# More places for the first attention pairs, and a planner that paces its transfers

## The chip, the cores and the metric

The kernel runs on one core of one Trainium2 chip. The metric is device time in microseconds (us) of one execution. TensorE is called PE below, its weight loads PEld; VectorE is DVE, ScalarE ACT, GpSimd POOL, SyncE SP.

## The reference

Attention with 4 batches, 8 heads, 768 positions and 64 channels, in float32. A position sees the 96 keys before it (itself included) and the 8 first keys of its batch. The result, 3072 rows of 512, goes through a two-layer network with a cosine gate.

```python
scores = scale * np.matmul(q, k.transpose(0, 1, 3, 2))
keep = is_global | is_local            # first 8 keys, or 0 <= rel < 96
scores = np.where(keep, scores + bias, -1e9)
a = np.exp(scores - max);  a = a / (a.sum(-1) + 1e-9)
x = np.matmul(a, v)                    # reshaped to (3072, 512)
h = x @ w_in                           # (3072, 2048)
out = (h * np.cos(h)) @ w_out          # (3072, 512)
```

## The kernel before

The 3072 rows are eight **chunks** of 384 (two for each batch). A chunk's attention is four **pairs** of heads; each pair gives 128 of the 512 columns of x. Numbered over all chunks there are 32 pairs.

A pair goes through these steps (the functions are `plan_loads`, `plan_unit`, `plan_values`): queries and keys arrive in a place of class `raw`, values in a place of class `v` (L438, L441); PE makes scores into a bank (L521 for the first eight pairs, in plain float32; L525 for the others, whose queries and keys are first split into two parts by `plan_split`, into a place of class `qk`); DVE folds (L538), adds distances and takes the minimum into a tile `tt` (L547); ACT takes exponentials (L572); DVE or POOL normalises (L595, L600); PE transposes (L664); DVE masks into a tile `pv` (L672, L677); PE multiplies by the values (L699); x is written in two parts, `xh` and `xl` (L253, L720).

The network is 128 **steps**, in each one block of 128 of the 2048 inner columns for one chunk. A step has 12 matmuls over x (L735, three for each pair's part of x, into one of two banks `ph`), then ACT L752, DVE L755, ACT L758 (cosine), DVE L793 (**the product**, after which the bank `ph` is free), a copy `gh` and DVE or POOL L802 `gl`, and at last 9 matmuls by w_out (L746). The order of the steps is in `PHASES`: chunk 0 with blocks 0 to 7, chunk 1 with blocks 0 to 15, chunk 0 with blocks 8 to 15, then the other chunks with all 16.

The weights arrive as 64-bit floats in 32 **tiles** of 512 KB (L372, 16 of w_in and 16 of w_out), and each is turned into two float32 parts by six operations on ACT, DVE and POOL (`plan_weights`; on DVE always the join L399, and at times L385 and L409).

The order on every engine is written by a planner at build time (`Plan.run`). It holds a list of operations with costs, due times and the places that each uses, and picks on each engine, in simulated time, the operation with the earliest due time that has its inputs and a free place. An operation that has a place of a class holds it until its last user is through. A place class has a list of names, `NT, NST, NPV, ...` of them; a name stands for a buffer. For SP the planner counts 470 ns for issuing a transfer, after which SP is free for the next; the data come later, one transfer behind the other (`extra`). Engines run what is written in that order. Where PE would stand idle in the first 45000 ns of the plan, matmuls of zeros are put in (`idle`, L1039).

A general fallback that stands behind the plan in the program is not run with these inputs.

## Time and profile before

| | us |
|---|---|
| three runs | 712.12, 712.63, 714.5 (median 712.63) |
| the profiled execution's own time | 714.17 |
| its span, from first to last instruction | 712.4 |
| PE busy | 688.6 (97%) |
| DVE busy | 518.8 (73%) |
| ACT busy | 450.9 (63%) |
| POOL busy | 135.8 (19%) |

The shares are means over the whole span. PE's busy time holds matmuls of zeros too. The rows on which the prediction rests stand in a section below, word for word.

### The profile page before, as it was taken

To read this page: it belongs to the slowest core of one execution; us is meant where nothing else is said; L and a number is where in the kernel's file an instruction comes from. 1 tells how busy PE (TensorE), PEld (TensorE's weight loads), DVE (VectorE), ACT (ScalarE), POOL (GpSimd) and SP (SyncE) were. 2 spreads that over 40 slices of the span, in tenths; PEclk is the share of its full clock that TensorE was granted. 3 is DMA by queue.
4 is the path that set the end of the run, shared out by engine and by line. 5 is a ranking of instruction groups with operands and counts; after the bars stand their busy time and mean duration, and the time that the engine had idled before them with its cause. 6 is when DMAs were issued, how large, how long until landed. Compare 5 with 4: busy or idle time off the path is not lost.

```text
span 712.4 us, 12947 instructions
## 1 busy us (share of the span) xinstructions
PE 688.6 (97%) x4483; PEld 598.4 (84%) x4483; DVE 518.8 (73%) x1542; ACT 450.9 (63%) x1130; POOL 135.8 (19%) x166
## 2 busy tenths in 40 slices
PE   7898999999999999999999999999999999999996
PEld 3657878988888888889889898888888888899884
DVE  7999999898767778487775887667785877743332
ACT  5799977786756576466664667566764666634342
POOL 4715656530002121011000121011000112000000
PEclk8999999999999999999999999999999999999999
DMA  8997210022420322132230422203122310001001
GB/s 303 407 351 209 59 48 24 1 59 64 112 68 29 83 65 65 48 103 60 56 71 15 112 61 58 59 19 106 42 68 67 90 49 2 1 1 45 1 0 50
DMA packets 32603, 55.74 MB, mean 78 GB/s; under 512 B 3472, under 2 KB 18192, under 8 KB 32528
## 3 DMA queue, kind: packets, MB, share of 16 engines
q1 hardware_dynamic: 32528, 54.82, 26.4%
q8 instruction: 37, 0.61, 0.4%
q14 instruction: 38, 0.31, 0.1%
HBM read 48.52 MB, written 6.29 MB: 77 GB/s over the span
## 4 chain that ended last, share of the span: by engine, by line
PE 72%; DVE 11%; ACT 8%; issue 2%; DMA 1%; POOL 0%; ACTq 0%; DVEq 0%; POOLq 0%; SPq 0%
PE bank L735 31%; PE bank L746 30%; PE bank L699 5%; PE bank L525 3%; ACT tt L572 2%; PE bank L664 2%; DVE wu L399 1%; ACT rr L758 1%; ACT L572 1%; DVE w L409 1%; DVE tt L547 1%; DVE gl L802 1%; DVE rr L755 1%; DVE qs L623 1%; DMA raw<-in_qk_dram 1%
## 5 line engine op out<-in xcount | busy, mean ns | idle before, releaser
L735 PE MATMUL bank<-xh,w 128*128 128x384 f32 x1024 | 298.1, 343 | 4.3 <-DVE rr L793 4.3
L746 PE MATMUL bank<-w,gh 128*128 128x512 f32 x768 | 243.6, 398 | 0.0
L735 PEld LDWEIGHTS bank<-xh,w 128*128 128x128 f32 x1024 | 189.1, 189 | 12.0 <-DVE rr L793 5.8
L735 PE MATMUL bank<-xl,w 128*128 128x384 f32 x512 | 173.3, 339 | 0.8 <-DVE xl L720 0.8
L746 PEld LDWEIGHTS bank<-w,gh 128*128 128x128 f32 x768 | 138.4, 188 | 21.5 <-ACT raw L394 0.3
L746 PE MATMUL bank<-w,gl 128*128 128x512 f32 x384 | 151.9, 396 | 0.0
L755 DVE SCALAR_TENSOR_TENSOR rr<-rr,bank 128x384 f32<-128x384 int32 x129 | 69.8, 542 | 102.6 <-ACT rr L752 102.2
L752 ACT ACTIVATE rr<-bank 128x384 int32<-128x384 f32 x129 | 62.1, 482 | 127.5 <-PE bank L735 124.5
L758 ACT ACTIVATE rr<-rr,half_pi 128x384 f32<-128x384 f32 x129 | 78.4, 613 | 43.0 <-DVE rr L755 41.4
L735 PEld LDWEIGHTS bank<-xl,w 128*128 128x128 f32 x512 | 96.8, 189 | 5.4 <-DVE xl L720 1.4
L793 DVE TENSOR_TENSOR rr<-bank,rr 128x384 f32<-128x384 f32 x129 | 70.5, 551 | 41.2 <-ACT rr L758 40.6
L572 ACT ACTIVATE tt<-tt,st 96x104 f32<-96x104 f32 (+1 forms) x256 | 94.2, 369 | 7.0 <-DVE st L547 6.4
L746 PEld LDWEIGHTS bank<-w,gl 128*128 128x128 f32 x384 | 72.1, 188 | 16.7
L257 POOL TENSOR_SCALAR ks<-raw 128x408 fp32r<-128x408 f32 (+1 forms) x35 | 21.1, 602 | 308.6 <-PE bank L525 291.6
L802 DVE TENSOR_TENSOR gl<-rr,gh 128x384 fp32r<-128x384 f32 (+1 forms) x113 | 65.9, 583 | 7.7 <-ACT gh L253 5.5
L253 ACT CAST gh<-rr 128x384 fp32r<-128x384 f32 (+1 forms) x99 | 50.2, 508 | 29.0 <-DVE rr L793 20.5
L547 DVE CUSTOM_DVE_ANT_0 tt<-bank,dd 96x104 f32<-96x104 f32 (+1 forms) x256 | 55.7, 257 | 3.0
L699 PEld LDWEIGHTS bank<-pv,v 104*64 104x64 f32 (+1 forms) x960 | 42.1, 138 | 12.5 <-issue 8.0
L525 PEld LDWEIGHTS bank<-ks,qs 128*96 128x96 f32 x384 | 45.8, 162 | 5.3 <-issue 0.8
L699 PE MATMUL bank<-pv,v 104*64 104x96 f32 (+1 forms) x960 | 48.3, 252 | 0.8 <-DMA raw<-in_qk_dram 0.4
L525 PE MATMUL bank<-ks,qs 128*96 128x200 f32 (+1 forms) x384 | 47.9, 255 | 0.5 <-DVE st L547 0.5
L572 ACT ACTIVATION_READ_ACCUMULATOR tt<-tt,st 96x1 f32 x256 | 47.9, 187 | 0.0
(96 smaller groups left out, 727.0 us busy)
## 6 DMA issues: line engine op xcount, KB each, us to landing
raw<-in_qk_dram SPq DMA_DIRECT2D x48, 224.0 KB
raw<-in_qk_dram SPq DMA_DIRECT2D x48, 198.0 KB
raw<-in_w_in_dram SPq DMA_DIRECT2D x16, 512.0 KB
raw<-in_w_out_dram SPq DMA_DIRECT2D x16, 512.0 KB
out_dram<-oo SPq DMA_DIRECT2D x24, 256.0 KB
v<-in_v_dram SPq DMA_DIRECT2D x16, 240.0 KB
v<-in_v_dram SPq DMA_DIRECT2D x16, 192.0 KB
raw<-in_qk_dram SPq DMA_DIRECT2D x4, 448.0 KB
```

The source lines that it names most:

```text
L253: self.nc.scalar.copy(out, x)
L525: nc.tensor.matmul(out, qs[:, m, q0], ks[:, k : k + w], start=m == 0, stop=m == 1)
L547: nc.vector.tensor_tensor_reduce(tt[t // 2].tile[:, t % 2, j, :w], ps.tile[:R, i * WIN : i * WIN + w], self.dd[:, v, :w], op0=ALU.add, op1 ...
L572: nc.scalar.activation(x, x, AF.Exp, bias=st.tile[:, c : c + 1], scale=-1.0, accum_out=st.tile[:, n2 + c : n2 + c + 1])
L699: nc.tensor.matmul(px.tile[j * D : (j + 1) * D, t * R : (t + 1) * R], vs.tile[:k, t + c, hs][:, j * D : (j + 1) * D], pv[:k, c, o : o + R] ...
L735: self.nc.tensor.matmul(ph[:, :CW], self.wi[f][:, w, kk * P : (kk + 1) * P], xx[:, kk, :], start=kk == 0 and m == 0, stop=kk == self.NK - ...
L746: self.nc.tensor.matmul(po, gg[:, ts], self.wo[f][:, w, :], start=start and m == 0, stop=stop and m == 2)
L752: self.nc.scalar.activation(r.bitcast(I32), ph, AF.Copy, scale=1.0 / TWO_PI, bias=0.25)
L755: self.nc.vector.scalar_tensor_tensor(r, r.bitcast(I32), -TWO_PI, ph, op0=ALU.mult, op1=ALU.add)
L758: self.nc.scalar.activation(r, r, AF.Sin, bias=self.half_pi)
L793: {DVE: dve}, lambda e, r=r, h=h: nc.vector.tensor_tensor(r(), h(), r(), op=ALU.mult), [o], [ph, rr]
L802: self.eng(e).tensor_tensor(g[1][:, cs], r(), g[0].bitcast(F32)[:, cs], op=ALU.subtract)
```

## The change

1. The first pairs may use more places. `HOMES = 7`: for the first seven pairs the classes `tt`, `v` and `pv` become `ttearly`, `vearly`, `pvearly`. `ttearly` is the five `tt` places and the two key places `k0`, `k1`; `vearly` is the three `v` places and the query place `q0`; `pvearly` the three `pv` places and `q1`. These four are otherwise first needed by the ninth pair.
2. For this the class `qk` is taken apart into `q` and `k`.
3. `NST` (statistics tiles) goes from 3 to 5.
4. `DEPTH = 3000`: in the plan SP is free again only when the transfers that have been issued end within 3000 ns.

```diff
-NT, NST, NPV, NX, NV, NRAW, NQK, NRR, NG = 5, 3, 3, 2, 3, 3, 2, 3, 2
+NT, NST, NPV, NX, NV, NRAW, NQK, NRR, NG = 5, 5, 3, 2, 3, 3, 2, 3, 2
+DEPTH = 3000
+HOMES = 7
...
                     if e == SP:
                         dma = max(end + 300, dma) + o.extra
+                        self.free[SP] = max(end, dma - DEPTH)
+                        heapq.heappush(heap, self.free[SP])
                         end = dma + 1400
...
+    def early(self, cls, n, pr):
+        return f"{cls}early" if n * self.NP + pr < HOMES else cls
...
-        vs = Slot("v", lambda i: self.work.tile([SLOT, 1 + CT, W], F32, name="v", tag=i))
+        vs = Slot(self.early("v", n, b2), lambda i: self.work.tile([SLOT, 1 + CT, W], F32, name="v", tag=i))
...
-        qk = Slot("qk", lambda i: [
-            self.work.tile([P, 2, CW], F32R, name="qs", tag=f"q{i}"),
-            self.work.tile([P, KW], F32R, name="ks", tag=f"k{i}"),
-        ])
+        qq = Slot("q", lambda i: self.work.tile([P, 2, CW], F32R, name="qs", tag=i))
+        kk = Slot("k", lambda i: self.work.tile([P, KW], F32R, name="ks", tag=i))
...
-                "tt": names("tt", NT), "st": names("st", NST), "qk": names("qk", NQK), "raw": names("raw", NRAW),
-                "v": names("v", NV), "pv": names("pv", NPV), "x": names("x", NX),
+                "tt": names("tt", NT), "st": names("st", NST), "q": names("q", NQK), "k": names("k", NQK), "raw": names("raw", NRAW),
+                "v": names("v", NV), "pv": names("pv", NPV), "ttearly": names("tt", NT) + names("k", 2),
+                "vearly": names("v", NV) + ["q0"], "pvearly": names("pv", NPV) + ["q1"], "x": names("x", NX),
```

The change moves instructions on every engine until about the 28th step; the last 102 products and what DVE does between them, and the last 101 steps on PE, stand in the same order as before. In the changed kernel the lines are 6 to 13 higher (L746 is the old L735, L757 the old L746, L710 the old L699, L675 the old L664, L534 the old L521, L444 and L447 the old L438 and L441, L493 the old L483, L378 the old L372).

On SP, before, the values of the fourth pair (`v`, 96x4x128) stand behind 18 of the 32 weight tiles:

```order
L372 DMA raw<-in_w_out_dram 128x1024 x3
L483 DMA raw<-in_qk_dram 128x896
L372 DMA raw<-in_w_out_dram 128x1024
L372 DMA raw<-in_w_in_dram 128x1024 x2
L438 DMA v<-in_v_dram 96x4x128
L441 DMA v<-in_v_dram 8x3x128
L372 DMA raw<-in_w_in_dram 128x1024 x2
```

On SP now:

```order
L444 DMA v<-in_v_dram 96x4x128
L378 DMA raw<-in_w_in_dram 128x1024
L493 DMA raw<-in_qk_dram 128x792
L447 DMA v<-in_v_dram 8x3x128
L444 DMA v<-in_v_dram 96x4x128
L447 DMA v<-in_v_dram 8x3x128
L378 DMA raw<-in_w_in_dram 128x1024 x3
L378 DMA raw<-in_w_out_dram 128x1024
L493 DMA raw<-in_qk_dram 128x896
```

The fourth pair's values (the second `v` here) now stand behind one weight tile. The queries and keys of the fifth to eighth pair (`raw`, 128x896) stand behind 5, 7, 10 and 12 tiles now; before, behind 5, 13, 27 and 31.

On PE, before, around the values' product of the fourth pair (L699, the fourth of its kind), which ends chunk 0's attention:

```order
L1039 MATMUL idle<-zeros 128x512
L699 MATMUL bank<-pv,v 64x96 x14
L521 MATMUL bank<-raw 96x200 x4
L664 MATMUL bank<-ident,tt 104x96 x4
L735 MATMUL bank<-xh,w 128x384
L735 MATMUL bank<-xl,w 128x384
```

On PE now, at the same place:

```order
L710 MATMUL bank<-pv,v 64x96 x14
L534 MATMUL bank<-raw 96x200 x4
L675 MATMUL bank<-ident,tt 96x96 x2
L675 MATMUL bank<-ident,tt 104x96 x6
L746 MATMUL bank<-xh,w 128x384
L746 MATMUL bank<-xl,w 128x384
L746 MATMUL bank<-xh,w 128x384 x2
L746 MATMUL bank<-xl,w 128x384
L746 MATMUL bank<-xh,w 128x384 x2
L746 MATMUL bank<-xl,w 128x384
L746 MATMUL bank<-xh,w 128x384
L710 MATMUL bank<-pv,v 64x96 x14
```

Now the fourth L710 follows the third with half a pair's scores, the fourth pair's transposes and nine matmuls of the first step between. Before, two and a half more score groups, the transposes, 18 step matmuls and 33 matmuls of zeros stand between the third and the fourth. In all there are 65 matmuls of zeros before and 30 now.

What DVE has ahead of it changes so (instructions on DVE ahead of four places, before and now; the two bold names are the product L793 and the last `xl` of a chunk, L720):

| DVE instruction (old line) | 4th **xl** | 5th **product** | 8th **product** | 11th **product** |
|---|---|---|---|---|
| fold L538 | 22, 18 | 24, 32 | 32, 32 | 32, 32 |
| minimum L547 | 44, 33 | 48, 64 | 64, 64 | 64, 64 |
| normalise L600 (L595) | 6, 4 (6, 4) | 8, 11 (6, 4) | 11, 11 (6, 4) | 11, 11 (6, 4) |
| mask L672 and L677, each | 9, 8 | 12, 14 | 16, 16 | 16, 16 |
| xl L720 | 4, 4 | 5, 7 | 7, 8 | 8, 8 |
| weights: join L399 | 8, 3 | 13, 13 | 16, 16 | 21, 18 |
| weights: L409 (L385) | 6, 1 (3, 1) | 7, 9 (4, 2) | 9, 11 (5, 2) | 11, 13 (8, 2) |
| gl L802 | 0, 0 | 3, 2 | 3, 5 | 6, 7 |
| query rest L623 | 0, 0 | 0, 0 | 0, 0 | 2, 0 |
| copies L255 and L490 | 0, 0 | 4, 2 | 8, 3 | 9, 4 |
| small L563, L580, L583, each | 5, 4 | 6, 7 (8, 8) | 8, 8 | 8, 8 |

On POOL there are 14 more instructions in all: 10 of them for weights (five of these L388), four for normalising. On ACT the table for exponentials or cosines is loaded 9 times ahead of the fifth cosine, 3 times before.

## Rows read from the trace of the kernel before

**Rows 1.** The page, its first part: busy time of each engine, its share of the span, and instructions.

```profile
PE 688.6 (97%) x4483; PEld 598.4 (84%) x4483; DVE 518.8 (73%) x1542; ACT 450.9 (63%) x1130; POOL 135.8 (19%) x166
```

**Rows 2.** Busy time by stretch. Columns: stretch and length, busy time of PE, PEld, DVE, ACT and POOL with their instructions, granted clock of TensorE (1.00 is 2.4 GHz), share of the DMA engines, GB/s.

```profile
0.00:38.00 38.00, 30.55 (x236) 19.75 (x237) 32.81 (x135) 26.11 (x91) 21.28 (x50) 0.91 0.97 350
38.00:57.00 19.00, 14.69 (x103) 8.44 (x103) 18.56 (x69) 17.77 (x48) 5.25 (x6) 1.00 1.04 370
0.00:74.37 74.37, 62.61 (x451) 43.95 (x451) 67.56 (x232) 59.87 (x171) 36.76 (x64) 0.93 0.89 304
0.00:113.64 113.64, 100.97 (x722) 75.04 (x722) 105.03 (x329) 91.40 (x246) 60.94 (x84) 0.95 0.66 219
57.68:61.10 3.42, 3.42 (x13) 3.42 (x11) 2.93 (x8) 3.03 (x12) 0.82 (x1) 0.50 1.09 264
20.00:57.68 37.68, 30.98 (x247) 19.92 (x246) 36.78 (x127) 34.26 (x99) 17.40 (x18) 1.00 1.04 380
114.24:704.00 589.76, 586.26 (x3755) 522.58 (x3756) 413.07 (x1211) 357.38 (x882) 74.30 (x83) 1.00 0.19 51
```

**Rows 3.** PE in order of time, from 38 us to the first L746. Columns: start and length in us, what it is, how many in the row, idle time before it and who ended that.

```profile
40.56 4.49 PE L1039 MATMUL idle<-zeros 128*128 128x512 bf16 x20
45.66 0.99 PE L521 MATMUL bank<-raw 64*96 64x200 f32 x8 [0.60 <-ACT raw L488]
46.58 0.54 PE L664 MATMUL bank<-ident,tt 96*104 96x96 f32 x4
46.96 2.11 PE L1039 MATMUL idle<-zeros 128*128 128x512 bf16 x9
48.99 1.39 PE L699 MATMUL bank<-pv,v 96*64 96x96 f32 x28
...
56.84 0.44 PE L735 MATMUL bank<-xh,w 128*128 128x384 f32 x1 [3.70 <-DVE rr L793]
...
62.67 0.62 PE L746 MATMUL bank<-w,gh 128*128 128x512 f32 x2
```

**Rows 4.** PE in order of time, the two last stops of more than half a us before the end of the start-up.

```profile
102.49 0.44 PE L735 MATMUL bank<-xl,w 128*128 128x384 f32 x1 [0.83 <-DVE xl L720]
...
114.24 0.44 PE L735 MATMUL bank<-xh,w 128*128 128x384 f32 x1 [0.63 <-DVE rr L793]
```

**Rows 5.** SP in order of time: issues of the fourth pair's values and of the last three `raw` loads of the first eight pairs.

```profile
23.61 0.33 SPq L483 DMA_DIRECT2D raw<-in_qk_dram  x1
...
28.70 0.33 SPq L438 DMA_DIRECT2D v<-in_v_dram  x1
...
45.45 0.35 SPq L483 DMA_DIRECT2D raw<-in_qk_dram  x1
...
54.07 0.35 SPq L483 DMA_DIRECT2D raw<-in_qk_dram  x1
```

**Rows 6.** DVE in order of time: the fourth xl, the fifth product and its successor, the eighth product, the eighth xl, the eleventh product with the join ahead of it.

```profile
51.35 0.58 DVE L720 TENSOR_TENSOR xl<-bank,xh 128x384 fp32r<-128x384 f32 x1
...
74.37 0.54 DVE L793 TENSOR_TENSOR rr<-bank,rr 128x384 f32<-128x384 f32 x1
74.83 0.55 DVE L755 SCALAR_TENSOR_TENSOR rr<-rr,bank 128x384 f32<-128x384 int32 x1
...
96.88 0.54 DVE L793 TENSOR_TENSOR rr<-bank,rr 128x384 f32<-128x384 f32 x1
...
101.90 0.54 DVE L720 TENSOR_TENSOR xl<-bank,xh 128x384 fp32r<-128x384 f32 x1
...
112.16 1.56 DVE L399 SCALAR_TENSOR_TENSOR wu<-raw 128x512 uint32<-128x512 uint32 x1
113.64 0.54 DVE L793 TENSOR_TENSOR rr<-bank,rr 128x384 f32<-128x384 f32 x1
```

**Rows 7.** Groups of DVE, one of POOL and three of ACT by line and shape, whole span. Columns: how many, busy time in us and mean ns of one, idle time before them and who ended it.

```profile
L547 DVE CUSTOM_DVE_ANT_0 tt<-bank,dd 96x104 f32<-96x104 f32 x224 | 50.0, 257 | 2.1
L538 DVE COPY_PREDICATED bank<-mine,bank 96x192 f32<-96x192 uint32 x96 | 32.9, 352 | 1.6 <-PE bank L521 0.8 <-PE bank L525 0.6
L388 POOL TENSOR_SCALAR raw<-raw 128x512 bf16<-128x512 bf16 x24 | 34.9, 1501 | 0.2
L600 DVE TENSOR_TENSOR tt<-tt,st 96x416 f32<-96x416 f32 x39 | 28.8, 754 | 0.1
L672 DVE TENSOR_TENSOR pv<-bank,others 104x384 f32<-104x384 f32 x48 | 26.2, 546 | 0.8 <-PE bank L664 0.8
L399 DVE SCALAR_TENSOR_TENSOR wu<-raw 128x512 uint32<-128x512 uint32 x32 | 24.6, 780 | 0.0
L409 DVE TENSOR_TENSOR w<-wu,w 128x512 fp32r<-128x512 f32 x17 | 13.2, 783 | 0.5 <-ACT w L253 0.5
L385 DVE TENSOR_SCALAR raw<-raw 128x512 uint16<-128x512 uint16 x8 | 6.0, 776 | 0.0
L572 ACT ACTIVATE tt<-tt,st 96x104 f32<-96x104 f32 x224 | 82.5, 369 | 4.0 <-DVE st L547 3.6
L572 ACT ACTIVATION_READ_ACCUMULATOR tt<-tt,st 96x1 f32 x256 | 47.9, 187 | 0.0
L758 ACT ACT_TABLE_LOAD x28 | 35.9, 1283 | 0.5
```

**Rows 8.** PE's steady prices, from the chain that ended last. Columns: start, us, what, how many.

```profile
114.24 2.35 PE bank L735 x12
116.59 2.08 PE bank L746 x9
118.67 2.12 PE bank L735 x12
120.80 2.09 PE bank L746 x9
232.35 1.48 PE bank L699 x32
```

**Rows 9.** The joins L399 and the normalising L600 on DVE over the span: shortest, median and longest in ns, first and last start.

```profile
L399 DVE SCALAR_TENSOR_TENSOR wu<-raw x32: 673/682/1559, 24.7 to 153.9; 128x512 uint32<-128x512 uint32 x32
L600 DVE TENSOR_TENSOR tt<-tt,st x39: 575/582/1746, 12.3 to 614.2; 96x416 f32<-96x416 f32 x39
```

More of the change, by code (lines that the diff above doesn't have):

```diff
@@ L268, in constants @@
         make_identity(nc, self.ident)
-        tile3 = lambda name, **kw: self.const.tile([R, 3, SLOT], F32, name=name, **kw)
-        self.dd = tile3("dd")
-        self.tmp = [tile3(f"tmp{i}", tag=f"tt{i}") for i in range(3)]
+        self.dd = self.const.tile([R, 3, SLOT], F32, name="dd")
+        self.tmp = [self.work.tile([R, 3, SLOT], F32, name=f"tmp{i}", tag=f"tt{i}") for i in range(3)]
         rel, col, _ = self.tmp
@@ L493, in plan_unit @@
             ready = [p.op({ACT: 520, DVE: 300, POOL: 490}, queries, [o], [raw], port=True)]
-            heads = [(raw, ready)] * 2
+            heads = [([raw], ready)] * 2
         else:
@@ L500, in plan_unit @@
         st = u["st"] = Slot("st", lambda i: self.work.tile([R, 6 * CT], F32, name="st", tag=i))
-        tt = u["tt"] = [Slot("tt", lambda i: self.const.tile([R, 2, 2, SLOT], F32, name="tt", tag=i)) for _ in range(0, CT, 2)]
+        tt = u["tt"] = [
+            Slot(self.early("tt", n, pr), lambda i: self.work.tile([R, 2, 2, SLOT], F32, name="tt", tag=i))
+            for _ in range(0, CT, 2)
+        ]
         lead = lambda t: first and t == 0
@@ L522, in score @@
                             continue
-                        qs, ks = heads[j][0].tile
+                        qs, ks = [x.tile for x in heads[j][0]]
                         for m in range(2):
@@ L530, in plan_unit @@
                 {PE: cost}, score, [o for j in js for o in heads[j][1]],
-                list(pss.values()) + [heads[j][0] for j in js[:1]] + [st, tt[h // 2]], mode="rows" if exact else None,
+                list(pss.values()) + heads[js[0]][0] + [st, tt[h // 2]], mode="rows" if exact else None,
             ))
@@ L618, in qhigh @@
         def qhigh(e):
-            nc.scalar.activation(qk.tile[0][:, 0], raw.tile[:, KW:], AF.Copy, scale=sc)
+            nc.scalar.activation(qq.tile[:, 0], raw.tile[:, KW:], AF.Copy, scale=sc)
         def qrest(e):
-            qs = qk.tile[0]
+            qs = qq.tile
             nc.vector.scalar_tensor_tensor(
@@ L627, in khigh @@
         def khigh(e):
-            self.copy(e, qk.tile[1][:, k0:], raw.tile[:, k0:KW])
+            self.copy(e, kk.tile[:, k0:], raw.tile[:, k0:KW])
         def krest(e):
-            ks = qk.tile[1]
+            ks = kk.tile
             self.eng(e).tensor_tensor(
@@ L637, in plan_split @@
         w = KW - k0
-        q = self.chain("qhigh", p.op({ACT: 410}, qhigh, loads, [raw, qk]))
-        q = p.op({DVE: 470}, qrest, [q], [raw, qk], port=True)
+        q = self.chain("qhigh", p.op({ACT: 410}, qhigh, loads, [raw, qq]))
+        q = p.op({DVE: 470}, qrest, [q], [raw, qq], port=True)
         k = self.chain("khigh", p.op(
             {ACT: 50 + w * 427 // 512, DVE: 70 + w * 265 // 512, POOL: 100 + w * 490 // 512},
-            khigh, loads, [raw, qk], port=True,
+            khigh, loads, [raw, kk], port=True,
         ))
-        k = p.op({DVE: 70 + w * 535 // 512, POOL: 100 + w * 1125 // 512}, krest, [k], [raw, qk], port=True)
-        return qk, [q, k]
+        k = p.op({DVE: 70 + w * 535 // 512, POOL: 100 + w * 1125 // 512}, krest, [k], [raw, kk], port=True)
+        return [qq, kk], [q, k]
     def plan_values(self, u):
@@ L654, in plan_values @@
             pt = self.bank(att)
-            pv = Slot("pv", lambda i: self.work.tile([P, 2, 4 * R], F32, name="pv", tag=i))
+            pv = Slot(self.early("pv", n, pr), lambda i: self.work.tile([P, 2, 4 * R], F32, name="pv", tag=i))
             lead = u["first"] and h == 0
```

## The prediction

> **What bounds the kernel now.** I read the page first. PE is busy 97% of the span [rows 1], so at first sight only PE's work counts, and the change takes none of the real work away. The table by stretch [rows 2] shows where the other 3% are. From 114.24 to 704 us PE is busy 586.26 of 589.76 us: there it is the bound, and it stands still for 3.5 us in all. Before, it is not: from 38 to 57 us PE is busy 14.69 of 19 us, a good part of that with matmuls of zeros, while DVE is busy 18.56 of 19. Up to the fifth product DVE has been busy 67.56 of 74.37 us, up to the eleventh 105.03 of 113.64. So **the start-up is bound by DVE, the rest by PE**, and the kernel's end is the moment at which PE stops waiting, plus work that is the same before and after.
>
> The timeline of PE shows what the start-up looks like [rows 3]. Twenty matmuls of zeros run at 40.56 us, then scores that waited for ACT, nine more zeros, and at 48.99 us the fourth pair's product with the values, the last thing that chunk 0 needs for its x. The values had only been asked for at 28.70 us [rows 5], behind 18 weight tiles. So chunk 0's last xl is written at 51.35 us [rows 6], PE then waits 3.70 us for a product, and the first L746 stands at 62.67 us. The eighth pair's load is issued at 54.07 us [rows 5], and PE stops for its xl at 102.49 us [rows 4]. The last such stop is at 114.24 us, for the eleventh product. From there it is 589.8 us to 704.
>
> **The change: where the time moves.** The work on each engine hardly changes; its order does. Since DVE is the bound of the start-up, I count what DVE has ahead of a place (the table in the section on the change), price the differences, and keep the time that DVE stood idle up to there.
>
> Fourth xl. Ahead of it are now fewer: 4 folds at 0.34, 11 minima at 0.22, 2 L600 at 0.74, 2 masks at 0.55, 5 joins at 0.77, 5 L409 at 0.78, 2 L385 at 0.75 (busy time by count) [rows 7], 2 L595 taken as 0.4 and 3 small ones as 0.2: 17.0 us. One instruction starts 0.08 us before the one ahead of it ends (74.37 + 0.54 against 74.83) [rows 6], which takes back up to 2.9 for the 36. I take 15.5: the fourth xl comes at about 36 instead of 51.35 us, and the first product, with some 6 us of DVE work behind it, at about 42.
>
> Fifth product. Now 8 folds more (2.7), 16 minima (3.6), 3 L600 (2.2), 4 masks (2.2), 2 xl (1.1), 2 L409 (1.6), 5 small (1.0); fewer by 2 L385 (-1.5), 2 L595 (-0.8), one gl and two copies at some 0.55 (-1.6): 10.5 us more, or 7.9 with the overlap. **I take 9.3**, the middle, since the small ones overlap more than the long ones. With the same idle time of DVE (74.37 - 67.56 = 6.8) the fifth product starts at 83.7, later than before, but much more of the second chunk's attention is done.
>
> From there PE decides. It starts the seventh step's matmuls 0.6 us behind the fifth product, as at 113.64 and 114.24 [rows 4, 6], so at 84.3. From the seventh to the thirteenth step's first matmul it now has six L735 groups at 2.12, five L746 groups at 2.09, one product with the values at 1.48 [rows 8] and four transposes (0.4): 25.0 us. So it comes to the thirteenth step at 109.3 instead of 114.24 us. Both kernels have the same work left there: **4.9 us earlier**.
>
> Is DVE ahead of PE all that way? Eighth product: now one xl, two gl and two L409 more, three L385, two L595 and five copies fewer, about -2: at 95, and PE wants it (its tenth step) at 96.8. Eighth xl: the table's differences put it near 92, PE wants it near 94. Eleventh product: three joins, six L385, two L623 and five copies fewer, two L409 and a gl more, about -8: at 105.6, wanted at 109. It holds, but by one to three us, so the size of the gain hangs on DVE's idle time at the fifth to eighth product. ACT has 16 exponentials (0.37 + 0.19) and six table loads (1.28) more ahead of the fifth cosine [rows 7], 16.6 us, and 13 weight operations fewer, of which I take half as much back: some 10 us on 59.87 [rows 2], 70 of 84 us. Near, but not the bound.
>
> Other edits together. Splitting `qk`, five `st` tiles and the four lent places cost no instruction; the lent places are wanted by the ninth pair, whose split follows the eighth pair's scores in any case. The order behind the 28th step is the same, so nothing is gained or lost there but what the 3.5 us of idle time hold; I take 0, bounds -1 and +1.
>
> Transfers. The eighth pair's load stands behind 12 tiles and needs a `raw` place that the fifth pair's scores free, some 2 us behind the fourth xl, at 38. About 10.6 MB stand ahead of it, 28 us at 380 GB/s [rows 2]. SP takes nothing past a waiting load, so the queue may run dry for some 10 us, and all weights behind it come later. What hides that: at that point 12 tiles are there and DVE joins its 13th only ahead of the fifth product, at 80 us. From 38 us on a tile lands each 1.4 us, so the 20th is there by 50 us. If that cover were gone, each tile would cost 1.4 us; I take 0.
>
> Sum: 714.17 - 4.9 = 709.3 us in terms of the profiled execution. That execution lies 1.5 above the median of the runs shown, 712.63; the forecast is against the median: **707.7 us**.
>
> Bounds. DVE's price 7.9 to 10.5: gain 6.3 to 3.6. DVE's idle time: 5.6 at least (that of the first 57 us) [rows 2], 8.6 at most (that up to the eleventh product): +1.2 to -1.8.
>
> POOL has 10 weight instructions more, five of them L388 at 1.45 us [rows 7], some 10 us in all; 13 of 32 tiles lie ahead of the fifth product, so 4.1 us of it. What POOL's presence costs DVE: the joins' mean is 780 against a median of 682 ns, L600's 754 against 582 [rows 7, 9], 0.10 x 32 + 0.17 x 39 = 9.8 us for 135.8 us of POOL, 7%; I take 0.3 us as inside the bounds. The Trainium skill ("SBUF — State Buffer", section "Who interferes with whom") says that a DVE instruction with two SBUF inputs and a POOL instruction that reads SBUF lock each other out, the later one for the whole of the other. The longest join, 1559 against 673 ns [rows 9], agrees with that; the medians say that it seldom happens. By that rule at its worst the 4.1 us would all fall on DVE, which is the first rival.
>
> **Rivals.**
> 1. *No change:* DVE loses up to the fifth product what the order gives. The place is DVE between the first and the fifth product, the price up to 4.1 us if all the added POOL work shuts DVE out, or as much idle time because DVE waits on ACT's six more table loads (1.3 us each). From 2.8 us on the change isn't measurable; 4.1 gives 711.8. For it: the margin of one us above. Against: DVE was idle only 5.6 us in 57 with all its inputs later than now.
> 2. *Slower:* PE's clock. Matmuls of zeros end early in the new order, and from the first to the fifth product (42.7 to 84.3) PE has 29 us of work: four L735 and four L746 groups, 20 scores at 0.25, 28 transposes at 0.1 [rows 3], three products with values. It stands still for 12.6 of 41.6 us. The rows show the granted clock at 0.50 (the level of 1.2 GHz) from 57.68 to 61.10, behind the stop of 3.70 us [rows 2, 3], and at 1.00 (2.4 GHz) over the 37.7 us before, with PE busy 82%. If all the 29 us ran at the lower level, PE would need 58, 16.4 us more than there are: 724 us. It decides from where more than 19.6 of the 29 us run so (12.6 idle, 4.9 gained, 2.1 to be measurable): 714.8. The Trainium skill ("TensorE: Matmul & The Clock Gate", section "HAM oscillation — how this bites in real kernels") tells of a kernel whose clock falls in the wait ahead of each tile; by that rule the trace's one stop agrees. Against it: such stops here are pieces of one or two us between attention and steps, and one fall costs 1.7 us, mostly inside the 12.6.
> 3. *More:* DVE's idle time stays at 5.6 and its price is the low one: 6.3 + 1.2 = 7.5, 705.1. For it: more places mean more work ready for DVE.
> 4. That the loads don't come earlier because they wait for `raw` all the same: true for the eighth pair (38 instead of 54.07), but the values of the fourth pair have no such wait. This only takes part of the third rival's gain.
>
> **How the numbers follow.** Forecast 0.68, more 0.12, no change 0.13, slower 0.07. A measurement here tells about 0.3%, 2.1 us, from no change, so faster is 0.80, within 0.13, slower 0.07. The range goes from 705.0 (the low bound) to 711.3 (gain 3.6 - 1.8 = 1.8, with 0.4 for POOL): it leaves out the slower case, half of "no change" and a little below, 0.17.
>
> **What would show it.** Right: the fourth xl near 36 us, the first product near 42, the fifth near 84, the thirteenth step's first matmul near 109, and 590 us from there to the last L757. DVE busy over 90% of the first 84 us. Wrong in size: DVE idle over 9 us at the fifth product. Wrong in kind: the granted clock at 0.50 for over 10 us between 45 and 84, or stops of PE for weights behind 90 us.

## The result, and the profile after

The changed kernel takes **716.94 us** (median of 4, 716.61 to 718.46) against 712.38 in the same series: ratio 1.0062, interval 1.0038 to 1.0087. A second series gave 716.55, ratio 1.0047 (1.0032 to 1.0063). It is slower by about 4 us; the forecast was 4.9 us faster. The profiled execution took 718.46 us, its span is 716.7.

Lines of the changed kernel that come up below, with the old ones: on DVE the product L804 (L793), xl L731 (L720), L766 (L755), gl L813 (L802), the join L405 (L399), L415 (L409), normalising L613 (L600), minima L560 (L547); on POOL the weights' **sign operation** L394 (L388). L260, L262 and L264 are copies.

The page's first part, after; beside [rows 1] POOL has 11.8 us more, PE and DVE about the same:

```profile
PE 687.2 (96%) x4448; PEld 600.5 (84%) x4448; DVE 521.0 (73%) x1531; ACT 450.9 (63%) x1129; POOL 147.6 (21%) x180
```

DVE after, in order of time: the fourth xl, the first and the fifth product, the eighth xl, the eighth and the eleventh product. In [rows 6] the same stand at 51.35, 74.37, 101.90, 96.88 and 113.64; the first product, not shown there, starts at 56.22 before.

```profile
36.38 0.57 DVE L731 TENSOR_TENSOR xl<-bank,xh 128x384 fp32r<-128x384 f32 x1
42.47 0.54 DVE L804 TENSOR_TENSOR rr<-bank,rr 128x384 f32<-128x384 f32 x1
...
85.31 0.54 DVE L804 TENSOR_TENSOR rr<-bank,rr 128x384 f32<-128x384 f32 x1
...
93.58 0.56 DVE L731 TENSOR_TENSOR xl<-bank,xh 128x384 fp32r<-128x384 f32 x1
...
98.87 0.55 DVE L804 TENSOR_TENSOR rr<-bank,rr 128x384 f32<-128x384 f32 x1
...
109.37 0.56 DVE L804 TENSOR_TENSOR rr<-bank,rr 128x384 f32<-128x384 f32 x1 [0.68 <-ACT rr L769]
```

So the early attention does come earlier, as forecast. Busy time by stretch after, columns as in [rows 2]:

```profile
0.00:85.31 85.31, 69.77 (x530) 51.73 (x530) 78.09 (x280) 69.00 (x202) 45.47 (x75) 0.88 0.85 278
0.00:109.38 109.38, 93.62 (x671) 73.47 (x672) 100.69 (x315) 89.29 (x241) 62.27 (x87) 0.89 0.68 220
45.00:90.00 45.00, 36.75 (x256) 29.90 (x255) 42.92 (x116) 39.41 (x100) 25.17 (x25) 0.85 0.74 252
90.00:140.00 50.00, 49.35 (x277) 44.17 (x275) 43.48 (x63) 36.92 (x72) 30.92 (x23) 1.00 0.08 21
112.71:708.20 595.49, 588.80 (x3756) 523.26 (x3755) 417.61 (x1212) 356.80 (x881) 85.38 (x93) 1.00 0.19 52
```

From the thirteenth step to some 0.9 us ahead of the start of the last L757 the changed kernel needs 595.5 us, where [rows 2] have 589.8 for the same stretch. It reaches the thirteenth step only 1.5 us earlier (112.73 against 114.24) and then loses 5.7. PE's stops are not over at the thirteenth step; five of them, columns as in [rows 3]:

```profile
75.97 0.44 PE L746 MATMUL bank<-xh,w 128*128 128x384 f32 x1 [1.34 <-DVE rr L804]
...
85.53 0.58 PE L675 MATMUL bank<-ident,tt 96*104 96x96 f32 x4 [2.03 <-ACT w L260]
...
140.82 0.59 PE L538 MATMUL bank<-ks,qs 128*96 128x200 f32 x4 [1.47 <-DVE st L560]
...
572.06 0.73 PE L757 MATMUL bank<-w,gh 128*128 128x512 f32 x2 [0.61 <-DVE oo L262]
...
573.58 0.45 PE L746 MATMUL bank<-xh,w 128*128 128x384 f32 x1 [0.56 <-DVE rr L804]
```

To place the loss I use a step's **level**: the start of its first matmul plus the PE work left from there, each matmul at its steady pitch. A level that rises by 1 us says that PE lost 1 us in between. One profiled execution each:

| kernel | 7th step | 13th | 18th | 28th | 100th | 104th | 128th |
|---|---|---|---|---|---|---|---|
| before | 698.8 | 701.8 | 701.6 | 702.9 | 706.2 | 706.3 | 705.2 |
| after | 698.8 | 700.3 | 700.2 | 704.1 | 708.5 | 710.5 | 709.4 |
| after, second run (6) | 699.1 | 699.7 | 699.6 | 703.8 | 708.3 | 709.7 | 708.7 |
| no pacing (1) | 694.8 | 704.6 | 705.8 | 706.3 | 710.0 | 710.2 | 709.1 |
| pacing only (2) | 692.0 | 699.3 | 699.2 | 703.1 | 707.7 | 707.9 | 706.9 |
| zeros in the stops (3) | 700.3 | 701.0 | 700.8 | 705.1 | 709.5 | 709.7 | 708.7 |
| after, no POOL sign (4) | 694.3 | 694.4 | 694.2 | 695.9 | 700.8 | 703.1 | 702.1 |
| before, no POOL sign (5) | 694.5 | 694.9 | 694.6 | 696.3 | 699.8 | 699.9 | 698.7 |
| split only (9) | 697.5 | 700.3 | 700.2 | 701.5 | 705.7 | 705.9 | 704.8 |
| output places (10) | 698.9 | 699.5 | 699.4 | 703.7 | 707.3 | 707.6 | 706.5 |
| late signs out (11) | 698.7 | 700.3 | 700.2 | 701.8 | 706.0 | 706.2 | 705.2 |
| no two-input POOL (12) | 697.8 | 698.2 | 697.9 | 699.8 | 703.2 | 703.3 | 702.2 |
| tt back (13) | 699.7 | 702.8 | 702.5 | 703.9 | 707.3 | 707.4 | 706.5 |
| new order, no lock (14) | 702.1 | 703.2 | 703.0 | 704.1 | 707.2 | 707.5 | 706.4 |

After against before: 1.5 won at the thirteenth step, 2.7 lost from there to the 28th, 1.1 to the 100th, 1.9 to the 104th: 4.2 us.

How far a single pair can be trusted, the table shows too. Three executions with the order of before (before, runs 9 and 13) stand at 701.8, 700.3 and 702.8 at the thirteenth step, three with the changed order (after, runs 6 and 10) at 700.3, 699.7 and 699.5. The means are 1.8 us apart, but executions of one order differ by up to 2.5, so a difference of 1 or 2 us at that step isn't told by one pair. The rise from the 13th to the 28th step is: 1.1 to 1.2 us in the first three, 3.8 to 4.2 in the others.

**Where DVE's time went.** From 132 to 141 us, POOL and then DVE, after:

```profile
132.80 1.67 POOL L394 TENSOR_SCALAR raw<-raw 128x512 bf16<-128x512 bf16 x1
...
136.74 1.67 POOL L394 TENSOR_SCALAR raw<-raw 128x512 bf16<-128x512 bf16 x1
```

```profile
133.17 1.57 DVE L405 SCALAR_TENSOR_TENSOR wu<-raw 128x512 uint32<-128x512 uint32 x1
134.66 0.54 DVE L766 SCALAR_TENSOR_TENSOR rr<-rr,bank 128x384 f32<-128x384 int32 x1
135.94 0.56 DVE L804 TENSOR_TENSOR rr<-bank,rr 128x384 f32<-128x384 f32 x1 [0.74 <-ACT rr L769]
136.41 0.78 DVE L813 TENSOR_TENSOR gl<-rr,gh 128x384 fp32r<-128x384 f32 x1
137.11 1.56 DVE L405 SCALAR_TENSOR_TENSOR wu<-raw 128x512 uint32<-128x512 uint32 x1
138.59 1.07 DVE L391 TENSOR_SCALAR raw<-raw 128x512 uint16<-128x512 uint16 x1
```

Both joins run while POOL's sign operation L394 does, and end 0.3 us behind it: 1.57 and 1.56 us instead of 0.68. They stand ahead of the folds and minima for which PE stops at 140.82. Up to 205 us, after, gl took 0.55 us with nothing of POOL's beside it (11 times) and 1.14 beside L394 (11 times), the join 0.68 and 1.34 (21 and 8 times); before there were 6 and 5 such collisions. Products and L766, with one input from a bank, took 0.53 to 0.56 either way. The Trainium skill ("SBUF — State Buffer", "Who interferes with whom") says the same: a DVE operation with two SBUF inputs contends with a POOL operation that reads SBUF, one with at most one SBUF input, outside its 2-port modes, doesn't.

Two inputs aren't the only case: the L391 shown, with one, took 1.07 us beside a copy of POOL's, and 0.74 at 81.61 us with POOL idle. Nor is the sign operation the only one of POOL's that does this. At the fifth product it is normalising; POOL and then DVE, after:

```profile
83.78 1.16 POOL L613 TENSOR_TENSOR tt<-tt,st 96x416 f32<-96x416 f32 x1 [0.41 <-DVE st L596]
```

```profile
84.12 1.27 DVE L613 TENSOR_TENSOR tt<-tt,st 96x416 f32<-96x416 f32 x1
```

DVE's L613, 0.58 us where it runs alone, ends at 85.39; the fifth product is next on DVE, and PE's transposes of `tt` follow at 85.53.

The planner isn't blind to such meetings. In the kernel's text, before and after, DVE's joins, gl, L415 and normalising (L608, L613) carry `port=True`, and `Plan.run` starts none of them in its simulated time while a POOL operation runs, nor the other way round (`self.port`). That the planner counts no stretch, as the expectations of runs 7, 8 and 12 have it, is true only in that it plans a wait in its place. But each engine keeps the plan's order, not its times: up to 205 us, 44 of 100 such operations on DVE ran beside one of POOL's after, and 32 of 101 before.

I call **stretch** the sum, over DVE's instructions, of length minus the median length of the same form with no POOL instruction beside it:

| up to product | before | after | after again | run 4 | run 5 | run 9 | run 11 | run 12 |
|---|---|---|---|---|---|---|---|---|
| fifth | 8.4 | 11.0 | 12.3 | 4.4 | 1.5 | 4.9 | 11.1 | 3.1 |
| thirteenth | 13.9 | 17.6 | 19.2 | 6.5 | 3.1 | 10.0 | 15.5 | 4.7 |
| 28th | 19.4 | 26.5 | 28.0 | 8.3 | 5.0 | 15.5 | 17.4 | 6.7 |

Without the stretch, DVE's work up to the 28th product is 5.6 us shorter after (sum of lengths 190.9 against 196.5); with it, DVE is busy 1.9 us longer (182.0 against 180.1).

### The profile page after: what moved, and what is told of

Read it like the earlier page. It is cut to its first block, busy times and chain, and to the rows that moved or that the text cites. A ratio compares the mean times of both kernels' runs of the same rounds, so it can differ in the third digit from the quotient of the medians.

```text
span 716.7 us, 12898 instructions
## 1 busy us (share of the span) xinstructions
PE 687.2 (96%) x4448; PEld 600.5 (84%) x4448; DVE 521.0 (73%) x1531; ACT 450.9 (63%) x1129; POOL 147.6 (21%) x180
## 4 chain that ended last, share of the span: by engine, by line
PE 70%; DVE 14%; ACT 7%; DMA 5%; issue 2%; POOL 1%; SPq 0%; ACTq 0%; DVEq 0%; POOLq 0%
PE bank L746 30%; PE bank L757 29%; PE bank L710 5%; PE bank L538 3%; DMA raw<-in_w_in_dram 3%; PE bank L675 3%; ACT tt L585 2%; DVE wu L405 2%; DVE tt L560 2%; DVE bank L551 1%; DVE w L415 1%; DVE qs L634 1%; ACT L585 1%; ACT rr L769 1%; DVE gl L813 1%
## 5 line engine op out<-in xcount | busy, mean ns | idle before, releaser
L746 PE MATMUL bank<-xh,w 128*128 128x384 f32 x1024 | 299.6, 346 | 2.2 <-DVE rr L804 2.2
L757 PE MATMUL bank<-w,gh 128*128 128x512 f32 x768 | 245.6, 401 | 0.6 <-DVE oo L262 0.6
L746 PEld LDWEIGHTS bank<-xh,w 128*128 128x128 f32 x1024 | 191.3, 191 | 9.6 <-DVE rr L804 3.3
L746 PE MATMUL bank<-xl,w 128*128 128x384 f32 x512 | 174.8, 341 | 0.2 <-DVE xl L731 0.2
L757 PEld LDWEIGHTS bank<-w,gh 128*128 128x128 f32 x768 | 138.2, 188 | 23.0 <-DVE oo L262 1.0
L757 PE MATMUL bank<-w,gl 128*128 128x512 f32 x384 | 151.5, 395 | 0.0
L766 DVE SCALAR_TENSOR_TENSOR rr<-rr,bank 128x384 f32<-128x384 int32 x129 | 69.8, 542 | 103.3 <-ACT rr L763 103.0
L746 PEld LDWEIGHTS bank<-xl,w 128*128 128x128 f32 x512 | 98.0, 191 | 4.3 <-DVE xl L731 0.4
L804 DVE TENSOR_TENSOR rr<-bank,rr 128x384 f32<-128x384 f32 x129 | 70.6, 551 | 38.2 <-ACT rr L769 37.8
L757 PEld LDWEIGHTS bank<-w,gl 128*128 128x128 f32 x384 | 72.2, 188 | 17.3
L264 POOL TENSOR_SCALAR ks<-raw 128x408 fp32r<-128x408 f32 (+1 forms) x34 | 20.5, 603 | 282.2 <-PE bank L538 268.0
L813 DVE TENSOR_TENSOR gl<-rr,gh 128x384 fp32r<-128x384 f32 (+1 forms) x114 | 69.2, 607 | 9.4 <-ACT gh L260 6.6
L260 ACT CAST gh<-rr 128x384 fp32r<-128x384 f32 (+1 forms) x97 | 49.1, 507 | 28.9 <-DVE rr L804 21.0
L560 DVE CUSTOM_DVE_ANT_0 tt<-bank,dd 96x104 f32<-96x104 f32 (+1 forms) x256 | 55.8, 257 | 2.9
L710 PEld LDWEIGHTS bank<-pv,v 104*64 104x64 f32 (+1 forms) x960 | 43.1, 141 | 13.8 <-issue 8.8
L710 PE MATMUL bank<-pv,v 104*64 104x96 f32 (+1 forms) x960 | 49.5, 255 | 2.6 <-DVE pv L688 1.1
L538 PEld LDWEIGHTS bank<-ks,qs 128*96 128x96 f32 x384 | 45.9, 162 | 6.3 <-issue 1.9
L538 PE MATMUL bank<-ks,qs 128*96 128x200 f32 (+1 forms) x384 | 48.1, 255 | 1.5 <-DVE st L560 1.5
```

What stands on the lines that cost most here:

```text
L260: self.nc.scalar.copy(out, x)
L538: nc.tensor.matmul(out, qs[:, m, q0], ks[:, k : k + w], start=m == 0, stop=m == 1)
L560: nc.vector.tensor_tensor_reduce(tt[t // 2].tile[:, t % 2, j, :w], ps.tile[:R, i * WIN : i * WIN + w], self.dd[:, v, :w], op0=ALU.add, op1 ...
L710: nc.tensor.matmul(px.tile[j * D : (j + 1) * D, t * R : (t + 1) * R], vs.tile[:k, t + c, hs][:, j * D : (j + 1) * D], pv[:k, c, o : o + R] ...
L746: self.nc.tensor.matmul(ph[:, :CW], self.wi[f][:, w, kk * P : (kk + 1) * P], xx[:, kk, :], start=kk == 0 and m == 0, stop=kk == self.NK - ...
L757: self.nc.tensor.matmul(po, gg[:, ts], self.wo[f][:, w, :], start=start and m == 0, stop=stop and m == 2)
```

## The experiments

Medians of 6 to 12 runs, ratios to the kernel before in the same series (712.8, 712.39, 713.44 and 713.7 us for runs 1 to 4, 5 to 8, 9 to 12, 13 and 14). The expectations weigh these theories: A, the pacing brings weights too late; B, the granted clock falls; C, POOL's weight operations stretch DVE's; D (run 5), the new order itself is worse.

**Run 1, no pacing.** `DEPTH = 10**9`.

> The changed kernel without the pacing of transfers (DEPTH so large that it never holds), the lent places kept. Theory A (pacing is the fault: weights land up to 20 us later, their joins end at 164 instead of 154 us, and DVE is late for the products behind the 13th step): weights are loaded by about 62 us again, the joins end near 154, the stop of 1.47 us at 140.8 is gone, and the time is 713 or less. Theory B (the granted clock: 23.9 us at 0.50 in the start-up against 10.2): the time follows the sum of the stretches at 0.50, whatever the transfers do; with under 12 us of them some 712, with 20 or more some 716. Theory C (POOL's added weight operations stretch DVE's): the time follows POOL's busy time up to 140 us; as long as it is near the changed kernel's, 716 to 717.

718.29 us, 1.0073 (1.0048 to 1.0099). Theory A as put falls: without pacing the lent places alone are no better. C's time (716 to 717) is exceeded too. The order that the planner finds then has 130.1 us of DVE's work (sum of lengths) ahead of the thirteenth product, where before has 120.2; the level there is 704.6.

**Run 2, pacing only.** `HOMES = 0`.

> The changed kernel with no lent places (HOMES = 0), the pacing kept. Theory A (pacing is the fault): slower than the kernel before by 3 to 5 us, 715 to 718, with late joins. Theory B (clock): by the stretches at 0.50 again; the first attention has its old places, so the clock should fall about as before (10 us in all) and the time be 711 to 714. Theory C (POOL): 712 to 714, by how many weight operations POOL has up to 140 us.

715.44 us, 1.0033 (1.0014 to 1.0052), in the range of theory A and above those of B and C. At the thirteenth step it is 2.5 us ahead of before; around 157 us PE waits 1.80 us for a minimum of DVE and then runs at a granted clock of 0.50 for 3.4 us, and at the 28th step the lead is gone. PE, and the stretch of low clock, columns as in [rows 3] and [rows 2]:

```profile
157.06 0.72 PE L538 MATMUL bank<-ks,qs 128*96 128x96 f32 x4 [1.80 <-DVE st L560]
```

```profile
157.31:160.72 3.41, 3.41 (x16) 3.37 (x15) 2.71 (x17) 3.40 (x16) 0.83 (x1) 0.50 0.03 5
```

Each half of the change loses on its own; both runs also have the moved tiles of run 9.

**Run 3, zeros in PE's stops.**

```diff
+WARM = {("score", 13): (4, ["b6"]), ("turn", 10): (9, ["b0"]), ("turn", 12): (6, ["b1"]), ("turn", 15): (8, ["b5"])}
```

> The changed kernel with 27 more matmuls of zeros (about 0.21 us each at a granted clock of 1.00, 5.8 us in all), in the four stops of PE at 50.1, 53.6, 65.3 and 85.5 us; nothing else differs. Theory B (clock): the stretches at 0.50 behind 45 us (6.8, 3.4 and 3.4 us) go, the fifth product comes 1 to 2 us earlier, the thirteenth step's first matmul near 109 to 110 instead of 112.7, and the time falls by 2 to 4 us, to 713 to 715. Theories A and C: the clock may stay at 1.00, but DVE decides from the 19th step on, and the time is within 1 us of the changed kernel's 716.9.

718.89 us, 1.0095 (1.0067 to 1.0124). The stretch from 45 to 90 us, columns as above:

```profile
45.00:90.00 45.00, 37.56 (x278) 27.90 (x275) 39.42 (x114) 38.07 (x95) 22.72 (x23) 0.96 0.75 244
```

The granted clock is 0.96 there instead of 0.85, and the time is above every forecast: the seventh step's matmuls start at 87.4 (85.9 after), the level at the thirteenth is 701.0 (700.3). That the zeros themselves delay something isn't ruled out here. But runs 6 and 10 have the order of after without more zeros, and by chance a higher clock. From the seventh to the thirteenth step's first matmul, after, in run 6 and in run 10 (0.50 falls into this stretch in the first alone, from 85.84 to 89.25):

```profile
85.91:112.73 26.82, 26.82 (x156) 24.33 (x154) 24.59 (x38) 22.86 (x44) 16.46 (x12) 0.94 0.03 9
```

```profile
86.19:112.08 25.89, 25.74 (x155) 22.70 (x154) 24.22 (x38) 22.26 (x43) 17.26 (x12) 1.00 0.04 11
```

```profile
86.02:111.94 25.92, 25.73 (x155) 22.71 (x154) 24.22 (x38) 22.29 (x43) 17.27 (x12) 1.00 0.04 12
```

The seventh step comes no earlier there (86.19 and 86.02), though the clock was 0.50 for 3.4 us between 45 and 85 us and not for 10.2: up to the fifth product a slow PE was hidden behind DVE. Behind it the low clock costs 0.9 us. Run 6 ends 0.7 below after in level, so theory B explains at most about 1 of the 4 us.

**Run 4, the changed kernel without POOL's sign operation; run 5, the kernel before without it.**

```diff
-                    nc.gpsimd.tensor_scalar(h[:, :, 1], h[:, :, 3], 0.0, 1.0, op0=ALU.mult, op1=ALU.mult)
+                    pass
```

> The changed kernel with the sign operation of the weights left out where POOL does it (its 1.5 us form, 26 of them up to 140 us): the weights' low words then have a wrong sign there; all other work and the order are the same. Theory C (POOL stretches DVE): DVE's operations are shorter, the joins near their median of 0.67 us, the eighteenth product starts 3 us or more earlier, the stops at 140.8 and 146.9 us go, and the time falls by 3 us or more, to 714 or less. Theory B (clock): the stretches at 0.50 stay, and so does the thirteenth step near 112; the time falls by less than 1.5 us. Theory A: the loads come no earlier, the joins end near 164 us still, and the time stays within 1 us.

> The kernel before with the same left out as from the changed kernel: the sign operation of the weights where POOL does it (24 of them, low words then have a wrong sign). If POOL's stretching of DVE is what separates the two kernels (theory C), the pair without it must come out as the order promised: the changed kernel without it (710.6) ahead of this one, so this one at 711 or more, since before loses less than the changed kernel by the stretch (13.9 against 17.7 us at the thirteenth product). If the stretch costs both the same (theory D: the new order itself is the worse one, wherever DVE's time goes), this kernel gains the same 6 us: 706 to 708, and the changed kernel stays 3 to 5 us behind.

710.58 us, 0.9965 (0.9946 to 0.9984), and 708.33 us, 0.9932 (0.9910 to 0.9954). Both leave work out, so they are tests and no candidates. Groups of DVE from 90 to 140 us, by line and shape, columns as in [rows 7]: before, after, and run 4 (whose lines are one lower than after's).

```profile
L399 DVE SCALAR_TENSOR_TENSOR wu<-raw 128x512 uint32<-128x512 uint32 x14 | 11.1, 806 | 0.0
L802 DVE TENSOR_TENSOR gl<-rr,gh 128x384 fp32r<-128x384 f32 x9 | 8.6, 961 | 0.0
```

```profile
L813 DVE TENSOR_TENSOR gl<-rr,gh 128x384 fp32r<-128x384 f32 x11 | 11.8, 1073 | 2.1 <-ACT gh L260 2.1
L405 DVE SCALAR_TENSOR_TENSOR wu<-raw 128x512 uint32<-128x512 uint32 x13 | 11.7, 916 | 0.0
L804 DVE TENSOR_TENSOR rr<-bank,rr 128x384 f32<-128x384 f32 x12 | 6.6, 553 | 4.1 <-ACT rr L769 4.1
```

```profile
L404 DVE SCALAR_TENSOR_TENSOR wu<-raw 128x512 uint32<-128x512 uint32 x12 | 8.0, 680 | 0.1
L812 DVE TENSOR_TENSOR gl<-rr,gh 128x384 fp32r<-128x384 f32 x11 | 7.6, 687 | 2.1 <-ACT gh L260 2.1
L803 DVE TENSOR_TENSOR rr<-bank,rr 128x384 f32<-128x384 f32 x11 | 6.1, 555 | 4.3 <-ACT rr L768 4.2
```

The sign operation costs the changed kernel 6 us and the one before 4. It is no cause of the changed kernel alone, as theory C wanted; but the 4 us between the two fall to 2.3, less than the 3 to 5 of theory D, and up to the 28th step nothing is left of them (levels 695.9 and 696.3). What remains comes later. The levels also say what the new order is worth without the sign operation: at the thirteenth step they differ by 0.5 us, within what two executions of one order differ by.

**Run 6, the changed kernel again.**

> The changed kernel itself, for a second profile and an interval in the same call. If the loss of 2.0 us between its steps 101 and 104 (a wait for an output transfer) belongs to the change, it stands in this profile too; if it falls now here, now there, it is absent or smaller, and the level at the end is 707 to 708 instead of 709.4. The level at the thirteenth step 700.3 and at the 28th 704.1 should come again within 1 us by either.

716.55 us. The loss around the 101st step stands again (1.4), so it isn't one execution's; levels at the 13th and 28th step came again within 0.6.

**Runs 7 and 8, sign on DVE alone**, from after and from before: `p.op({DVE: 650}, wsign, ...)`.

> The changed kernel with the sign operation allowed on DVE alone (0.75 us there, 29 instances moved, planned anew). Theory C: POOL's rows up to 140 us fall by some 40 us and the stretch from 26 to under 10 us up to the 28th product, while DVE's own work grows by 29 x 0.75 = 22 us: a loss of about 4 us, 718 to 722. The planner, which counts no such stretch, gives this order 7.1 us more than the changed kernel: 722 to 725.

> The kernel before with the sign operation allowed on DVE alone (24 instances moved, planned anew). Theory C: stretch from 19.4 to under 8 us up to the 28th product, DVE's own work 24 x 0.75 = 18 us more, spread over 28 steps: 713 to 717. The planner gives this order 1.3 us more than the kernel before: 714 if its times held.

715.69 us, 1.0042 (1.0022 to 1.0062), and 713.55, 1.0011 (0.9998 to 1.0024). Stretch up to the 28th product falls to 6.5 and 9.7 (under 10 and under 8 were expected), DVE's own work grows by 29 and 22 us of length, and neither time moves by more than 1.3: what a stretch costs and what it costs to avoid it in this way are about equal. Run 7 came out below both of its forecasts.

**Run 9, split only:** `HOMES = 0` and `DEPTH = 10**9`; the order of before on every engine. The diff in the section on the change leaves out a line that this run keeps: the `tt` tiles (and with them the first mask tiles `tmp`) come from another pool.

```diff
-        tt = u["tt"] = [Slot("tt", lambda i: self.const.tile(...
+            Slot(self.early("tt", n, pr), lambda i: self.work.tile(...
```

> The changed kernel without lent places (HOMES = 0) and without pacing: what is left is the class qk taken apart, NST = 5 and the place of the first tiles in memory. Every engine's instructions stand in the order of the kernel before. If only the order counts: 712.4, the level of before at each step within 0.5 us. The kernels built from the changed one lose 1.0 to 1.2 us more between the 28th and the 100th step than those built from the one before, in matmuls that each take some ns longer; if that comes with the new layout and not with the order, this kernel loses it too: 713.4 to 713.8.

713.79 us, 1.0011 (0.9997 to 1.0024). The times can't tell 1 us. The trace can: PE, first matmuls of the 28th and the 100th step.

```profile
188.39 0.34 PE L746 MATMUL bank<-xh,w 128*128 128x384 f32 x1
...
562.82 0.42 PE L746 MATMUL bank<-xh,w 128*128 128x384 f32 x1
```

**Run 13, tt back:** as run 9, with `self.tmp` and `tt` from `self.const` instead of `self.work`.

> The kernel of the run with the split alone (order of before on every engine), with the tt tiles and the first mask tiles allocated in the pool in which they were before. If the 1.1 us between the 28th and the 100th step comes from the moved tiles, all of which shift what lies behind them, it is gone here: the stretch from the 28th to the 100th step's first matmul 373.5 us instead of 374.4, and the time 0.5 to 1.2 below that run. If it comes from the five st tiles or the split places, the stretch stays 374.4.

712.74 us, 0.9994 (0.9974 to 1.0014). The same two matmuls:

```profile
190.76 0.34 PE L746 MATMUL bank<-xh,w 128*128 128x384 f32 x1
...
564.44 0.42 PE L746 MATMUL bank<-xh,w 128*128 128x384 f32 x1
```

374.4 us with the tiles moved, 373.7 with them back (before 373.6, after 374.6). It sits in matmuls that follow another of the same kind: 545 of L757 take 128.7 to 128.8 us in the traces of before and of runs 5, 8, 12 and 13, and 129.3 to 129.6 in those of after and of all other runs; 759 of L746 take 135.2 to 135.5 and 135.7 to 135.8. No trace lies between. So the move of the tt tiles to another memory pool costs 1.1 us in the trace (the two times, 713.79 and 712.74, are a like distance apart, with overlapping intervals), 0.6 to 1.5 ns in each of these matmuls; which operand's place does it was not tried.

**Run 10, more output places.**

```diff
-            oo = Slot("wu", lambda i: self.work.tile([P, 512], F32, name="oo", tag=i))
+            oo = Slot("oo", lambda i: self.work.tile([P, 512], F32, name="oo", tag=i))
...
+                "oo": names("wu", 2) + names("part", NTOK),
```

> The changed kernel, with five places for the output rows (the two of wu and the three of part) where it had two. Up to the 28th step the order is the same. The third output tile of a chunk then doesn't wait for the transfer of the first. If the loss of 1.4 to 2.0 us at the 101st step is that wait, it is gone here and the time is 715.0 to 716.0; if another thing is late there, 716.5 as in the changed kernel.

714.81 us, 1.0024 (1.0011 to 1.0037). DVE at the 100th step, after, and in run 10:

```profile
568.93 0.55 DVE L766 SCALAR_TENSOR_TENSOR rr<-rr,bank 128x384 f32<-128x384 int32 x1
571.31 0.69 DVE L262 COPY oo<-bank 128x512 f32<-128x512 f32 x1 [1.83 <-DMA out_dram<-oo]
571.92 0.55 DVE L262 CAST xh<-bank 128x384 fp32r<-128x384 f32 x1
```

```profile
567.06 1.24 DVE L766 SCALAR_TENSOR_TENSOR rr<-rr,bank 128x384 f32<-128x384 int32 x2
568.72 0.56 DVE L262 CAST xh<-bank 128x384 fp32r<-128x384 f32 x1 [0.42 <-PE bank L710]
```

After, the third output tile waits for the transfer of the first, two products behind it on DVE wait too, and PE stops twice. With more places the level rises by 0.3 instead of 1.4 to 2.0. The time is a little below the forecast: from the 28th to the 100th step the level rises by 3.6 instead of 4.4, and PE's stops of 0.43 us at 318.0 and 485.5 us, which before has too (0.41 and 0.44), are gone. Why the transfer lands late at the 100th step stays open: the wait stands in after, its second run and run 4, but not in runs 3 and 11, which have the same order there and the same places. DVE in run 11, the same copy:

```profile
567.05 0.69 DVE L262 COPY oo<-bank 128x512 f32<-128x512 f32 x1
```

So these 1.9 us fall in some executions of the changed order and not in others; how often isn't known.

**Run 11, late signs out:** POOL's last 12 of 29 sign operations left out.

> The changed kernel with POOL's sign operation left out for the last 12 of its 29 (those that start behind 100 us; the low words of these weights then have a wrong sign); the first 17 stay. Theory C for the second half of the loss: up to the tenth step nothing changes and the 13th step's level stays near 700; from there to the 28th the level rises by 1.4 us, as in the two kernels without any such operation, and not by 3.8: 714.0 to 714.8. If DVE's lateness at the 19th to 24th step comes from the late weights or the order, the level still rises by 3 to 4 us: 716 to 717.

713.98 us, 1.0008 (0.9990 to 1.0025). From the 13th to the 28th step the level rises by 1.5 instead of 3.8. That settles this part of the start-up: of the 2.7 us lost there, 2.3 go with POOL's late sign operations, by way of DVE.

**Run 12, no two-input weight work on POOL,** from the kernel before:

```diff
-p.op({ACT: 580, DVE: 500, POOL: 700}, wlow, ...)
+p.op({ACT: 580, POOL: 700}, wlow, ...)
-p.op({DVE: 650, POOL: 1310}, wsign, ...)
+p.op({DVE: 650}, wsign, ...)
-p.op({ACT: 580, DVE: 345, POOL: 640}, wbias, ...)
+p.op({ACT: 580, POOL: 640}, wbias, ...)
-p.op({DVE: 600, POOL: 1260}, wrest, ...)
+p.op({DVE: 600}, wrest, ...)
```

> A try for a better kernel, from the one before: the weights' sign and last subtraction on DVE alone, their low words and bias on ACT or POOL; POOL then has no sign operation of 1.5 us and no weight operation with two inputs. DVE has 24 x 0.65 + 15 x 0.68 = 26 us more, less the low words and bias that it no longer does, and some 14 us less stretch by the 28th product. The planner, without the stretch, gives it 1.5 us more than the kernel before. If the stretch weighs as in the other runs: 708 to 713; if DVE's own work weighs more: 714 to 718.

**710.45 us, 0.9961 (0.9946 to 0.9976)**: 0.4% faster than before, and so faster than both kernels, though the planner gives it 1.5 us more than before.

**Run 14, the same edit and the output places of run 10 on the changed kernel.**

> The changed kernel with the weights' sign and last subtraction on DVE alone, low words and bias on ACT or POOL (as in the run from the kernel before that took 710.45), and five places for the output rows. If the new order is worth its 4.9 us where POOL doesn't stretch DVE, less 1.1 for the layout: 707 to 709. If the order gains nothing once both are free of the stretch, as the pair without POOL's sign operation says (levels 694.4 and 694.9 at the thirteenth step): 710.5 to 713.

714.71 us, 1.0021 (1.0006 to 1.0036), slower than either case expected. Levels at the thirteenth step are 703.2 here and 698.2 in run 12: with under 5 us of stretch up to that product in both, the order planned with the new places and the pacing gains nothing and loses 5 us there. Both orders are planned anew, and this one has some 135 us of DVE's work (sum of lengths without the stretch) ahead of the thirteenth product, run 12 some 130.

## Why the prediction was wrong

- **Fourth xl, first product: right.** 36.4 and 42.5 for 36 and 42, and for the reason given: DVE is busy 15.3 us less ahead of the fourth xl (15.5 taken). The fifth product was forecast at 83.7 and came at 85.3: DVE's busy time ahead of it grew by 10.5 us (9.3 taken, 2.6 of the 10.5 are stretch), its idle time is 7.2 (6.8 taken).
- **POOL's stretch, taken as 0.3 us: this step failed, in size and in reach.** The stretch is 2.6 us more up to the fifth product, 3.7 up to the thirteenth, 7.1 up to the 28th. I spread a mean (7% of POOL's time) over the 13 tiles ahead of the fifth product. What counts is which operation meets which: 12 of the 29 L394 start behind 100 us. The first rival named the mechanism, its place too narrowly.
- **"Both kernels have the same work left", bounds -1 to +1: this step failed most.** The rest took 5.7 us more. I checked that DVE is ahead of PE up to the eleventh product, and took the stops behind it as before's. DVE is the bound again around the 19th and 24th step: 2.7 us, 2.3 of them shown to be POOL's late sign operations (run 11). The moved tt tiles, a line of the change that I gave no price, cost 1.1 us (runs 9 and 13). A wait for an output transfer costs 1.9 (run 10); it isn't in every execution (runs 3 and 11), so that it belongs to the change is not shown.
- **The gain of 4.9 at the thirteenth step: 1.5.** 1.6 us went with the later fifth product; from the seventh to the thirteenth step PE took 26.8 us instead of 25.0. Of these 1.8 us, 0.9 are the low clock behind the fifth product (runs 6 and 10 need 25.9); the other 0.9 stay open. Runs 4 and 5 suggest that the gain hangs on DVE being late in the kernel before: without POOL's sign operation 0.5 us of it are left, which one pair of executions can't tell from nothing.
- **The slower rival (clock)** foresaw the sign but not the cause: the low clock came, 13.6 us of it between 45 and 90 us, and cost nothing up to the fifth product and 0.9 us behind it. That the time came out on this rival's side is luck.
- **Loads waiting for weights:** no stop of PE behind 90 us is put down to weights. The one of 2.03 us at 85.53 is put down to ACT's `w`, but it ends at transposes of `tt`, 0.14 us behind the end of DVE's L613, so DVE's normalising is the likelier cause (not tested).

## What to carry to other kernels

An order that is free of collisions in a plan's simulated time isn't free of them on the chip, since only the order is kept. Here a join or gl of DVE that met POOL's sign operation took twice as long on average (1.34 against 0.68 us, 1.14 against 0.55). So count meetings in the trace, not means, and follow the critical engine until it is out of reach for good, not until the first crossing. In the plan's own times the 128th step of the changed kernel starts 3.5 us ahead of before (671.4 against 674.9), on the chip 4 behind, and the one order with all the work in it that beat both (run 12) was 1.5 us behind before in the plan. A line that only moves a buffer is a change too: compare the pitch of the steady part.

## Not expected of the hardware

- Matmuls of the steady part take 0.6 to 1.5 ns more each when the tt tiles are allocated from another pool (runs 9 and 13).
- The same order has 15.5 us of stretch in one profiled execution (run 9) and 19.4 in another (before): collisions fall differently each time. The runs of before spread from 709.3 to 716.7 us.
